# Later chunks of 384 tokens, issued from a second table of steps, in a linear-attention and feed-forward kernel

## The chip, the cores and the metric

The kernel runs on one core of one Trainium2 chip. The core has a matrix engine (PE in the profile; its weight loads are PEld), a vector engine (DVE), a scalar engine (ACT), a general engine (POOL), and SP, which issues most DMAs. Each engine takes its own instructions in order and waits on semaphores for the others. The metric is the device time of one execution in microseconds (us); the median over several runs counts.

## The reference

There are 8 batches of 8 heads, 576 tokens each, head width 64, and 128 random features. All is float32.

```python
def phi(x):
    proj = np.einsum('bhsd,md->bhsm', x, omega)
    sq = np.sum(x * x, axis=-1, keepdims=True) / 2.0
    h = proj - sq
    h = h - np.max(h, axis=-1, keepdims=True)
    return np.exp(h) / np.sqrt(m)
...
kv = np.einsum('bhsm,bhsd->bhmd', k_p, v)
z = np.sum(k_p, axis=2)
num = np.einsum('bhsm,bhmd->bhsd', q_p, kv)
den = np.einsum('bhsm,bhm->bhs', q_p, z)[..., None] + 1e-06
...
h = x @ w_in
g = h - np.tanh(h)
return (g @ w_out)
```

The attention output (4608 tokens by 512) is `x`; `w_in` is 512 by 2048, `w_out` 2048 by 512.

## The kernel before, in words

The 2048 columns between the two weight matrices are cut into 16 slices of 128. Each float32 operand of the large products is kept as a high and a low part of a faster type, and a product is made of three matmuls: high by high, high by low, low by high. For a slice of weights and a chunk of tokens that gives 12 matmuls into `h` (4 blocks of the 512 inputs by 3, line 373) and 3 matmuls for each 128 tokens into the output bank `po` (lines 403 to 405). Between them lies a chain on two engines, the tile's **g chain**: tanh on ACT (`g`, line 379), `h - tanh` on DVE (line 381), the high part on ACT (`gh`, 384), the low part on DVE (`gl`, 387). `g` is one tile; `gh` and `gl` have two buffers.

Tokens are worked in chunks. Chunks 0 and 1 (512 tokens together) form a first stage whose order is written out in a table (`ORDER`, one step per word, each step on one engine). There the weights are also read and decoded. All of this first stage, up to slice 13, stands in that table. The later stage takes slices 14 and 15 of it and then chunks 2 to 17, 256 tokens each: a loop over chunks and over pairs of slices, so that one **unit** is 24 matmuls of 256 columns into one bank `h`, and 12 matmuls of 512 columns into two banks `po`. Units alternate on PE: the 24 matmuls of the next unit stand before the 12 of this one.

Beside it runs the attention for later chunks. A **q unit** (chunk, pair of heads `c`) loads 256 queries, splits them, makes the features (`pj_q`, line 177), the row minima and exponentials, the denominators, turns the result by four transposes (`pt`, line 325), splits it into `qh` on ACT (329) and `ql` on DVE (330), and multiplies by the key-value matrix in the **numerators** (`pn`, lines 336 and 337: for each of two heads one matmul with `qh` and one with `ql`, cut where a batch ends inside the chunk). Then `xs` is put together (340 to 343) and split into the chunk's input `xh` and `xl` (349, 350). A **k unit** (batch, pair of heads) does the same kind of work for the keys of a batch. These units are Python generators; `beat()` advances each by one yield at fixed points of the loop, and the dictionary `start` says at which beat a unit begins. The instructions so emitted are then put in order for each engine by the framework's scheduler. While the banks of the first stage are in use, features, transposes and numerators share one PSUM bank, `pj0`.

Of the kernel before, what the change touches and what calls it, by code (L numbers as in the profile page):

```python
# [78 lines left out]


@with_exitstack
def favor_attention_ffn(ctx: ExitStack, tc: tile.TileContext, qT, kT, va, vt, omT, w, out):
# [77 lines left out]
    def split_rows(x, f):  # L160

        copy(mode["hi"], x[0:D, 0, :], f[0:D])
        copy(mode["hi"], x[D:P, 1, :], f[D:P])
        nc.vector.tensor_sub(x[D:P, 0, :], f[0:D], x[0:D, 0, :].bitcast(F32))
        nc.vector.tensor_sub(x[0:D, 1, :], f[D:P], x[D:P, 1, :].bitcast(F32))

    def features(lhs, name):

# [4 lines left out]
        for g in range(0, n, 2):
            m = min(2, n - g)
            pj = ps.tile([P, 2, 2 * M], F32, tag=bank("pj"), name=f"pj_{name}_{g}")
            for i in range(m):
                nc.tensor.matmul(pj[:, i], lhs[g + i], om2, start=True, stop=True)  # L177
# [13 lines left out]
    def k_unit(b, c):  # L191

        f = att("kf", [P, S], F32, f"kf_{b}_{c}")
        load(f, kT[c, :, b * S : (b + 1) * S])
        yield from k_single(b, c, f)

    def k_single(b, c, f):


        n = f"{b}_{c}"  # L200
        v = att("vr", [P, 9, D], F32, f"v_{n}")
        nc.sync.dma_start(v, vt[b - 2, c])
        yield
        x = att("kx", [P, 2, S], F32R, f"kx_{n}")
        split_rows(x, f)
        yield
        xf = x.rearrange("p h s -> p (h s)")
        tiles = [xf[:, t * P : (t + 1) * P] for t in range(9)]
        pk = ps.tile([P, 2, 2, M], F32, tag=bank("pk"), name=f"pk_{n}")
        zs = att("zs", [P, 2, M], F32, f"zs_{n}")  # L210

        def split(ph, t, n_t):

            ku = []
            for g in range(0, n_t, 2):
                w = min(2, n_t - g)
                k = att("khl", [P, 2, 2, M], F32R, f"khl_{n}_{t + g}")
                u = att("vhl", [P, 2, 2, D], F32R, f"vhl_{n}_{t + g}")
                nc.vector.tensor_copy(k[:, :w, 0], ph[:, g : g + w])  # L219
                nc.gpsimd.tensor_sub(k[:, :w, 1], ph[:, g : g + w], k[:, :w, 0].bitcast(F32))  # L220
                if n_t > 1:
                    parts = [(slice(0, P), slice(0, w), slice(t + g, t + g + w))]
                else:
                    parts = [(slice(D * h, D * h + D), h, t) for h in range(2)]
                    nc.gpsimd.memset(u[0:D, 1].bitcast(F32), 0.0)
                    nc.gpsimd.memset(u[D:P, 0].bitcast(F32), 0.0)
                for p, i, j in parts:
                    nc.gpsimd.tensor_copy(u[p, i, 0], v[p, j])  # L228
                    nc.vector.tensor_sub(u[p, i, 1], v[p, j], u[p, i, 0].bitcast(F32))
                ku += [(k[:, i if n_t > 1 else 0].rearrange("p a m -> p (a m)"),  # L230
                        u[:, i].rearrange("p a d -> p (a d)")) for i in range(2)]
            return ku

        def kv(h, ku, first, last):
            for i, (k, u) in enumerate(ku):
                nc.tensor.matmul(pk[:, h].rearrange("p a m -> p (a m)"), u, k,  # L236
                                 start=first and i == 0, stop=last and i == len(ku) - 1)

        def zsum(ph, h):
            zt = att("c1", [P, 2, M], F32, f"zt_{n}_{h}")  # L240
            nc.gpsimd.tensor_add(zt, ph[:, 0:2], ph[:, 2:4])
            nc.gpsimd.tensor_add(zs[:, h], zt[:, 0], zt[:, 1])

        pa = features(tiles[0:4], f"ka{n}")
        yield
        ku = split(pa, 0, 4)
        zsum(pa, 0)
        yield
        pm = features(tiles[4:5], f"km{n}")
        kv(0, ku, True, False)  # L250
        yield
        km = split(pm, 4, 1)
        yield
        pb = features(tiles[5:9], f"kb{n}")
        kv(0, km[:1], False, True)
        kv(1, km[1:], True, False)
        yield
        zsum(pb, 1)
        nc.gpsimd.tensor_add(zs[0:D, 0], zs[0:D, 0], pm[0:D, 0])
        nc.gpsimd.tensor_add(zs[D:P, 1], zs[D:P, 1], pm[D:P, 0])  # L260
        ku = split(pb, 5, 4)
        yield
        kv(1, ku, False, True)
        zhl = att("khl", [P, 2, 2, M], F32R, f"zhl_{n}")
        nc.vector.tensor_copy(zhl[:, 0], zs)
        nc.gpsimd.tensor_sub(zhl[:, 1], zs, zhl[:, 0].bitcast(F32))
        c1 = att("c1", [P, 2, M], F32, f"c1_{n}")
        nc.scalar.copy(c1, pk[:, :, 0])
        nc.vector.tensor_add(c1, pk[:, :, 1], c1)
        yield  # L270
        for h in range(2):
            nc.tensor.transpose(pk[:, 0, h], c1[:, h], ident)
        for i in range(2):
            nc.tensor.matmul(pk[:, 1].rearrange("p h m -> p (h m)"), ones,
                             zhl[:, i].rearrange("p h m -> p (h m)"), start=i == 0, stop=i == 1)
        kvt = att("kvs", [P, 2, D], F32, f"kvs_{n}")
        nc.scalar.copy(kvt, pk[:, 0, :, D:])
        nc.vector.tensor_add(kvt, pk[:, 0, :, 0:D], kvt)
        zb = att("zb", [P, 2, M], F32, f"zb_{n}")
        nc.scalar.copy(zb, pk[:, 1])  # L280
        w = att("kvw", [P, 4, D], F32R, f"kvw_{n}")
        nc.scalar.copy(w[:, 0::3, :], kvt)
# [139 lines left out]


    need = {b: (b * S) // TC for b in range(B)}
    xdone = {}
    x2 = {}
    gens = []

# [401 lines left out]
```

## Time and profile before

| what | us |
|---|---|
| median of 3 runs | 1056.81 (1055.3 to 1058.27) |
| the profiled execution | 1051.56 |
| its span, first to last instruction | 1049.8 |
| PE busy | 1032.1 |
| DVE busy | 803.9 |
| ACT busy | 678.4 |
| POOL busy | 278.5 |

All times of single instructions come from this one execution. Matmuls overlap, since one starts while the last is still leaving the array, so a matmul's own duration is longer than the distance to the next one; the distance between starts is what a matmul costs a full PE. I call it the pitch.

### The profile page before, as it was taken

The numbers are of one execution on the slowest core, as the hardware profiler recorded it, in microseconds if no ns is written. First come the engines' busy times: TensorE is split into PE (matmuls) and PEld (weight loads), VectorE is DVE, ScalarE is ACT, GpSimd is POOL, SyncE is SP. The second block draws the span as 40 slices with busy tenths as digits, with TensorE's granted clock in tenths as the row PEclk, the third lists the DMA queues.
The fourth block names the chain that finished last, engine by engine and source line by source line (L and its number), as shares of the span: only waits on it lengthen the run. The fifth ranks groups of instructions, "written<-read, shape, count | busy, mean of one in ns | idle before, by whom it ended". The sixth has DMA issues, their size and how long they took to land.

```text
span 1049.8 us, 20079 instructions
## 1 busy us (share of the span) xinstructions
PE 1032.1 (98%) x6908; PEld 935.6 (89%) x6908; DVE 803.9 (77%) x2761; ACT 678.4 (65%) x1730; POOL 278.5 (27%) x445
## 2 busy tenths in 40 slices
PE   8899999989999999999999999999999999999998
PEld 7677888989999999999999998999999999999997
DVE  6997776775788876789889888998888887666522
ACT  7998655664676755676677677676667675555422
POOL 0344760001233310234333323333333341000000
PEclk9999999999999999999999999999999999999999
DMA  8999662010111100010111111111101010100000
GB/s 234 291 249 268 127 156 66 32 41 1 29 54 33 42 23 31 23 53 23 53 29 54 33 54 34 44 39 34 54 24 52 25 40 7 35 12 21 1 21 21
DMA packets 43462, 64.67 MB, mean 62 GB/s; under 512 B 18656, under 2 KB 28000, under 8 KB 41312
## 3 DMA queue, kind: packets, MB, share of 16 engines
q1 hardware_dynamic: 38672, 38.19, 12.4%
q10 hardware_dynamic: 2384, 16.81, 4.6%
q0 software_dynamic: 2304, 8.39, 4.2%
q8 instruction: 55, 0.90, 0.4%
q14 instruction: 47, 0.39, 0.1%
HBM read 45.55 MB, written 9.44 MB: 52 GB/s over the span
## 4 chain that ended last, share of the span: by engine, by line
PE 87%; DVE 4%; ACT 4%; DMA 2%; POOL 1%; issue 1%; ACTq 0%; DVEq 0%; POOLq 0%
PE h L373 37%; PE po L403 11%; PE po L404 11%; PE po L405 11%; PE pj_q L177 3%; PE pt L325 2%; PE pk L236 2%; PE pn L337 2%; PE pn L336 2%; DMA w<-a 2%; ACT k_phi L491 1%; PE pj_ka L177 1%; PE pj_kb L177 1%; DMA q_f<-qT 1%; POOL a L638 1%
## 5 line engine op out<-in xcount | busy, mean ns | idle before, releaser
L373 PE MATMUL h<-xh,w 128*128 128x256 f32 (+1 forms) x2176 | 448.7, 291 | 2.7 <-DMA w<-a 1.9
L373 PEld LDWEIGHTS h<-xh,w 128*128 128x128 f32 x2176 | 355.0, 191 | 12.8 <-DMA w<-a 2.8
L373 PE MATMUL h<-xl,w 128*128 128x256 f32 (+1 forms) x1088 | 316.7, 291 | 1.0 <-DVE xl L350 1.0
L373 PEld LDWEIGHTS h<-xl,w 128*128 128x128 f32 x1088 | 207.7, 191 | 7.4 <-DVE xl L350 1.2
L403 PE MATMUL po<-w,gh 128*128 128x512 f32 x544 | 213.8, 393 | 0.0
L404 PE MATMUL po<-w,gh 128*128 128x512 f32 x544 | 213.4, 392 | 0.0
L405 PE MATMUL po<-w,gl 128*128 128x512 f32 x544 | 211.6, 391 | 0.0
L384 ACT CAST gh<-g 128x512 fp32r<-128x512 f32 x144 | 89.7, 623 | 96.3 <-DVE g L381 93.6
L379 ACT ACTIVATE g<-h 128x512 f32<-128x512 f32 x144 | 85.7, 595 | 95.2 <-PE h L373 84.3
L381 DVE TENSOR_TENSOR g<-h,g 128x512 f32<-128x512 f32 x144 | 98.8, 686 | 61.5 <-ACT g L379 60.2
L387 DVE TENSOR_TENSOR gl<-g,gh 128x512 fp32r<-128x512 f32 x144 | 109.9, 763 | 46.3 <-ACT gh L384 44.3
L405 PEld LDWEIGHTS po<-w,gl 128*128 128x128 f32 x544 | 102.3, 188 | 21.2
L403 PEld LDWEIGHTS po<-w,gh 128*128 128x128 f32 x544 | 102.5, 188 | 16.7 <-issue 0.3
L404 PEld LDWEIGHTS po<-w,gh 128*128 128x128 f32 x544 | 102.5, 188 | 15.5
L185 ACT ACTIVATE phi_q<-phi_q,nb_q 128x128 f32<-128x128 f32 x240 | 78.8, 392 | 4.1 <-DVE nb_q L181 4.0
L220 POOL TENSOR_TENSOR khl<-phi_ka,khl 128x256 fp32r<-128x256 f32 x40 | 31.5, 796 | 176.0 <-DVE khl L219 168.3
L330 DVE TENSOR_TENSOR ql<-pt,qh 128x512 fp32r<-128x512 f32 x60 | 41.2, 686 | 38.2 <-ACT qh L329 38.0
L315 DVE CUSTOM_DVE_ANT_0 junk<-phi_q,zb 128x128 f32<-128x128 f32 (+1 forms) x200 | 59.9, 300 | 11.6 <-DVE dn L315 0.5
L181 DVE CUSTOM_DVE_ANT_0 phi_q<-pj_q,phi_q 128x128 f32<-128x128 f32 x240 | 55.9, 283 | 7.2 <-ACT phi_q L178 7.2
L638 POOL TENSOR_SCALAR a<-a 128x1024 f32<-128x1024 f32 x14 | 53.9, 3852 | 20.8 <-ACT a L627 14.4
L329 ACT CAST qh<-pt 128x512 fp32r<-128x512 f32 x60 | 34.9, 582 | 37.7 <-PE pt L325 37.5
L228 POOL CAST vhl<-v 128x128 fp32r<-128x128 f32 (+1 forms) x120 | 37.7, 314 | 78.6 <-PE pk L236 73.1
(158 smaller groups left out, 1835.9 us busy)
## 6 DMA issues: line engine op xcount, KB each, us to landing
raw<-w ACTq DMA_DIRECT2D x16, 1024.0 KB, 6.0
out<-o SPq DMA_DIRECT2D x36, 256.0 KB, 2.0
w<-a POOLq DMA_DIRECT2D x16, 512.0 KB, 6.1
qf<-qT SPq DMA_DIRECT2D x60, 128.0 KB, 2.1
kf<-kT SPq DMA_DIRECT2D x20, 288.0 KB, 2.8
v<-vt SPq DMA_DIRECT2D x20, 288.0 KB, 2.8
v<-va SPq DMA_DIRECT2D x12, 320.0 KB, 4.9
k_f<-kT SPq DMA_DIRECT2D x12, 288.0 KB, 4.3
```

The lines of the kernel that those rows point to most:

```text
L181: nc.vector.tensor_tensor_reduce(ph[:, j], pj[:, i, :M], ph[:, j], scale=-SCALE, scalar=3.0e38, op0=ALU.add, op1=ALU.min, accum_out=nb[:, ...
L185: nc.scalar.activation(ph[:, j], ph[:, j], AF.Exp, bias=nb[:, j : j + 1], scale=-1.0)
L315: nc.vector.tensor_tensor_reduce(bank("junk")[r], ph[r, i], kvs[b, c][1][r, h], scale=1.0, scalar=EPS, op0=ALU.mult, op1=ALU.add, accum_ou ...
L373: nc.tensor.matmul(o, w_, x, start=i == 0, stop=i == len(prods) - 1)
L379: nc.scalar.activation(g, p, AF.Tanh)
L381: nc.vector.tensor_sub(g, p, g)
L384: nc.scalar.copy(gh, g)
L387: nc.vector.tensor_sub(gl, g, gh.bitcast(F32))
L403: nc.tensor.matmul(po[t], h, wt[f][:, 0, DM:], start=first, stop=False)
L404: nc.tensor.matmul(po[t], h, wt[f][:, 1, DM:], start=False, stop=False)
L405: nc.tensor.matmul(po[t], l, wt[f][:, 0, DM:], start=False, stop=last)
L638: engine.tensor_scalar(u["af"], u["af"], -TOP, TOP, op0=ALU.max, op1=ALU.min)
```

## The change

From token 768 on, chunks hold 384 tokens instead of 256: 10 chunks of 384 in place of 15 of 256, while chunk 2 keeps its 256. A unit of such a chunk is one slice: 12 matmuls of 384 columns into `h` and 9 of 512 columns into three banks `po`. A q unit has 384 queries: six features, two banks of three transposes, and numerators of 384 columns. Generators, beats and the scheduler are gone from the later stage. All its steps stand in a second table, `LATER`, of some 4200 words in the order of a list scheduling, and each engine takes its instructions in that order. The table also names the PSUM bank of each product. Several small tiles (`g`, `gh`, `gl`, `xs`, the output's copies) become fixed places in three larger ones, `zf`, `zr` and `xb`; the inputs of odd and even chunks lie in `xa` and `xb`.

```diff
+TW = 384
+START = [0, TC, 2 * TC, *range(3 * TC, NT, TW)]
+NCH = len(START)
...
+LATER = """
+x.h0 q30.ld f0d.o0 x.h1 x.l0 x.h2 x.l1 f0e.h0.6 x.h3 x.l2 x.l3 f0e.h1 q30.sa f0d.o1 q30.sv f0e.th f0d.o2 f0e.g q31.ld
...
+fce.th fcd.o1 fce.g fce.gh fcd.o2 fce.gl fcf.h0.7 fcf.h1 fce.o0 fcf.th fce.o1 fcf.g fcf.gh fce.o2 fcf.gl fcf.o0 fcf.o1
+sc.c0.0 fcf.o2 sc.d0 sc.c1.0 sc.d1 sc.c2.0 sc.d2
...
+    def slices_of(ch, s):
+        return (2 * s, 2 * s + 1) if ch == 2 else (s,)
...
+            for i, (w_, x) in enumerate(prods):
+                if ch == 2 or half is None or half == i // 6:
+                    nc.tensor.matmul(o, w_, x, start=i == 0, stop=i == len(prods) - 1)
...
+        def turned(slot, h):
+            u["pt", h] = ps.tile([P, TW], F32, tag=BANKS[slot], name=f"pt_{n}_{h}")
+            for t in range(WB):
+                nc.tensor.transpose(u["pt", h][:, t * P : (t + 1) * P], u["ph"][:, 2 * t + h], ident)
+
+        def q_hi(h):
+            u["qh", h] = ak.tile([P, TW], F32R, tag="qh", name=f"qh_{n}_{h}")
+            nc.scalar.copy(u["qh", h], u["pt", h])
+
+        def q_lo(h):
+            u["ql", h] = ak.tile([P, TW], F32R, tag="ql", name=f"ql_{n}_{h}")
+            nc.vector.tensor_sub(u["ql", h], u["pt", h], u["qh", h].bitcast(F32))
+
+        def numerators(slot, h):
+            u["pn", h] = ps.tile([P, TW], F32, tag=BANKS[slot], name=f"pn_{n}_{h}")
+            for b, s, e in pieces:
+                w = kvs[b, c][0][:, h * P : (h + 1) * P]
+                nc.tensor.matmul(u["pn", h][:, s:e], w, u["qh", h][:, s:e], start=True, stop=False)
+                nc.tensor.matmul(u["pn", h][:, s:e], w, u["ql", h][:, s:e], start=False, stop=True)
...
+    def f_unit(ch, s):
+        u = {}
+        n = 4 if ch < 3 else WB
+        g = zf[:, 0:n]
+        gh, gl = (zr[:, k + s % 2 * 4 : k + s % 2 * 4 + n] for k in (0, 8))
...
+    def issue(order, makers):
+        units = {}
+        for token in order.split():
             name, step_, *slot = token.split(".")
             if name not in units:
                 units[name] = makers[name[0]](*(int(x, 16) for x in name[1:]))
             units[name][step_](*(int(x) for x in slot))
...
+    with tc.manual_schedule():
+        issue(ORDER, dict(k=native_k, q=native_q, d=decoder, f=feed))
...
+        issue(LATER, dict(k=k_unit, q=q_unit, f=f_unit, s=s_unit, x=x2_unit))
```

In the table `f3a.h0` and `f3a.h1` are the first and last six matmuls into `h` of chunk 3, slice 10; `th`, `g`, `gh`, `gl` its chain and `o0` to `o2` its output blocks. `q31.z0`, `a0`, `l0`, `m0` are the transposes, `qh`, `ql` and numerators of the first head of pair 1 in chunk 3.

The order on PE at three places. First, where chunk 3 begins. In the order before, `pt_3` are the transposes of pair 3 of chunk 3, `po` the outputs of chunk 2, and `h_0` the first unit of chunk 3:

```order
L403 MATMUL po_2_1991<-w_1638,gh_6_2454 128x512
L404 MATMUL po_2_1991<-w_1638,gh_6_2454 128x512
L325 MATMUL pt_3_2272<-ident,phi_q_3_2147 128x128 x4
L405 MATMUL po_2_1991<-w_1638,gl_6_2456 128x512
L403 MATMUL po_2_1991<-w_1682,gh_6_2454 128x512
L404 MATMUL po_2_1991<-w_1682,gh_6_2454 128x512
L405 MATMUL po_2_1991<-w_1682,gl_6_2456 128x512
L373 MATMUL h_0_2574<-xh,w_508 128x256
L373 MATMUL h_0_2574<-xl,w_508 128x256
```

The order after on PE at the same place, from the numerators of pair 3, second head (`pn_3_1`), to the first unit of chunk 3; between the rows shown stand the 12 matmuls of `po_0` and `po_1` with `w_1608` and `w_1649`:

```order
L625 MATMUL pn_3_1_2625<-qh_3_1_2585,k_kvw 128x384
L626 MATMUL pn_3_1_2625<-ql_3_1_2603,k_kvw 128x384
L698 MATMUL pk_1_2634<-khl_1_A_2560,vhl_1_A_2484 128x256 x2
L458 MATMUL pj_k_1_M<-om,kx_1_2338 128x256
L570 MATMUL po_0_2045<-w_1608,zr 128x512
...
L698 MATMUL pk_1_2634<-khl_1_A_2628,vhl_1_A_2600 128x256 x2
L458 MATMUL pj_k_1_B_2675<-om,kx_1_2338 128x256 x2
L458 MATMUL pj_k_1_B_2679<-om,kx_1_2338 128x256 x2
L547 MATMUL h_0_2684<-xa,w_508 128x384 x6
L698 MATMUL pk_1_2634<-khl_1_M,vhl_1_M 128x256 x2
L547 MATMUL h_0_2684<-xa,w_508 128x384 x6
```

All numerators of chunk 3 now stand ahead of its first unit, with 12 output matmuls between; before, the transposes of the last pair stood just ahead of it.

Second, between transposes and numerators of a q unit. In the order before on PE, the transposes of pair 0 of the next chunk, where fewest matmuls follow them before the numerators (which come 21 rows below the transposes):

```order
L325 MATMUL pt_0_2509<-ident,phi_q_0_2401 128x128 x4
L373 MATMUL h_0_2574<-xh,w_508 128x256
L373 MATMUL h_1_2665<-xh,w_743 128x256
L373 MATMUL h_0_2574<-xl,w_508 128x256
L373 MATMUL h_0_2574<-xh,w_508 128x256
L373 MATMUL h_0_2574<-xh,w_1068 128x256
L373 MATMUL h_0_2574<-xl,w_1068 128x256
```

The order after on PE, pair 1 of chunk 3, where fewest follow (`pt_1_0` and `pt_1_1` are the transposes of its two heads):

```order
L611 MATMUL pt_1_0_2152<-zf,phi_q_1_1942 128x128 x3
L611 MATMUL pt_1_1_2159<-zf,phi_q_1_1942 128x128 x3
L570 MATMUL po_1_2070<-w_743,zr 128x512
L571 MATMUL po_1_2070<-w_743,zr 128x512
L572 MATMUL po_1_2070<-w_743,zr 128x512
L570 MATMUL po_1_2070<-w_782,zr 128x512
L571 MATMUL po_1_2070<-w_782,zr 128x512
L572 MATMUL po_1_2070<-w_782,zr 128x512
L625 MATMUL pn_1_0_2178<-qh_1_0_2163,k_kvw 128x384
L626 MATMUL pn_1_0_2178<-ql_1_0_2174,k_kvw 128x384
```

The numerators of a head have moved up to directly behind nine short rows; the work of a whole unit no longer lies between.

Third, the last chunk, on PE in the order after, from the 12 matmuls of slice 14 to the outputs of slice 13 and the matmuls of slice 15:

```order
L547 MATMUL h_14_11859<-xa,w_1708 128x384 x3
L547 MATMUL h_14_11859<-xb,w_1708 128x384 x9
L570 MATMUL po_0_11530<-w_1649,zr 128x512
L571 MATMUL po_0_11530<-w_1649,zr 128x512
L572 MATMUL po_0_11530<-w_1649,zr 128x512
L570 MATMUL po_1_11536<-w_1649,zr 128x512
L571 MATMUL po_1_11536<-w_1649,zr 128x512
L572 MATMUL po_1_11536<-w_1649,zr 128x512
...
L547 MATMUL h_15_11885<-xa,w_1740 128x384 x3
L547 MATMUL h_15_11885<-xb,w_1740 128x384 x9
L570 MATMUL po_0_11530<-w_1708,zr 128x512
```

The alternation of units is kept, but between a unit's `h` and its `po` stand 9 matmuls of 512 columns and 12 of 384, where 12 of 512 and 24 of 256 stood.

More of the change, by code (lines that the diff above doesn't have):

```diff
@@ L188, in favor_attention_ffn @@
     kvf = {}
     kvs = {}
[L191 to L282, printed above, removed]
-        nc.vector.tensor_sub(w[:, 1:3, :], kvt, w[:, 0::3, :].bitcast(F32))
-        kvs[b, c] = (w.rearrange("p a d -> p (a d)"), zb)
@@ new lines, in ffn_g, with ffn_out @@
+    def ffn_g(ch, s, p):
+        n = 4 if ch < 3 else WB
+        p = blocks(p)[:, 0:n]
+        g = zf[:, 0:n]
+        gh, gl = (zr[:, k + s % 2 * 4 : k + s % 2 * 4 + n] for k in (0, 8))
+        nc.scalar.activation(g, p, AF.Tanh)
+        yield
+        nc.vector.tensor_sub(g, p, g)
+        yield
+        nc.scalar.copy(gh, g)
+        yield
+        nc.vector.tensor_sub(gl, g, gh.bitcast(F32))
+        yield gh, gl
+    def ffn_out(ch, s, gh, gl, only=None):
+        po = pos[ch]
+        for t in range(len(po)) if only is None else (only,):
+            for j, f in enumerate(slices_of(ch, s)):
+                first, last = f == 0, f == NF - 1
+                nc.tensor.matmul(po[t], gh[:, 2 * j + t], wt[f][:, 0, DM:], start=first, stop=False)
+                nc.tensor.matmul(po[t], gh[:, 2 * j + t], wt[f][:, 1, DM:], start=False, stop=False)
+                nc.tensor.matmul(po[t], gl[:, 2 * j + t], wt[f][:, 0, DM:], start=False, stop=last)
@@ L395, in ffn_out @@
-    def ffn_out(ch, s, gh, gl):
-        po = pos[ch]
-        for t in range(len(po)):
-            for j in ((t // 2,) if ch == 0 else range(2)):
-                f = s if ch == 0 else 2 * s + j
-                h = gh[:, j, t % 2 * P : (t % 2 + 1) * P]
-                l = gl[:, j, t % 2 * P : (t % 2 + 1) * P]
-                first, last = f == 0, f == NF - 1
-                nc.tensor.matmul(po[t], h, wt[f][:, 0, DM:], start=first, stop=False)
-                nc.tensor.matmul(po[t], h, wt[f][:, 1, DM:], start=False, stop=False)
-                nc.tensor.matmul(po[t], l, wt[f][:, 0, DM:], start=False, stop=last)
@@ new lines, in q_unit @@
+        st = dict(ld=ld, sa=sa, sv=lambda: split_lo(u["x"], u["f"]), xh=lambda: x_hi(ch, c, xs), xl=lambda: x_lo(ch, c, xs))
+        for t in range(WB):
+            lhs = lambda t=t: [u["x"][:, h, t * P : (t + 1) * P] for h in range(2)]
+            st.update(pair(u, str(t), lhs, 2 * t, f"q{n}", lambda slot: ak.tile([P, 2 * WB, M], F32, tag=f"phq{slot}", name=f"phi_q{n}")))
+            st[f"d{t}"] = partial(den, t)
+        for h in range(2):
+            for k, f in dict(n=norm, z=turned, a=q_hi, l=q_lo, m=numerators, ta=x_part, tv=x_sum).items():
+                st[f"{k}{h}"] = partial(f, h=h)
@@ L420, in out_tiles @@
-    def out_tiles(ch, tags=("po0", "po1")):
-        pos[ch] = [ps.tile([P, DM], F32, tag=t, name=f"{t}_{ch}") for t in tags]
[L424 to L427, printed above, removed]
-    def tick(new=(), force=False):
-        assert gens or not force
-        gens[:] = [g for g in gens if next(g, gens) is not gens]
-        for kind, i, c in new:
-            gens.append((k_unit if kind == "k" else q_unit)(i, c))
-            next(gens[-1])
+                nc.vector.tensor_copy(u[t], blocks(pos[ch][t]))
+            else:
+                nc.scalar.copy(u[t], blocks(pos[ch][t]))
@@ L438, in tile_at, with send, x2_unit @@
+        def send(t):
+            r = START[ch] + t * P
+            nc.sync.dma_start(blocks(out[r : r + P, :]), u[t])
+        st = {}
+        for t in range(4):
+            st.update({f"c{t}": partial(copy_out, t=t), f"d{t}": partial(send, t)})
+        return st
+    def x2_unit():
+        st = {}
+        for c in range(NC):
+            st.update({f"h{c}": lambda c=c: x_hi(2, c, x2[c]), f"l{c}": lambda c=c: x_lo(2, c, x2[c])})
+        return st
     def tile_at(kind, slot, shape, dtype, name):
```

719 lines of the change are left out of this document (520 added, 199 removed).

## Prediction

> **What bounds the kernel now.** I read the page's busy line first, then the windows (busy time of each engine in stretches), the chain that ended last, and PE's timeline where a window is not full.
>
> ```profile
> span 1049.8 us, 20079 instructions
> PE 1032.1 (98%) x6908; PEld 935.6 (89%) x6908; DVE 803.9 (77%) x2761; ACT 678.4 (65%) x1730; POOL 278.5 (27%) x445
> ```
>
> The windows; columns: stretch, length, busy us of PE, PEld, DVE, ACT, POOL, then PE's granted clock.
>
> ```profile
> 150.00:200.00 50.00, 50.00 (x291) 44.10 (x290) 33.44 (x106) 30.57 (x69) 3.31 (x5) 1.00 0.23 60
> 200.00:250.00 50.00, 47.32 (x304) 42.85 (x303) 35.92 (x129) 28.22 (x71) 2.95 (x4) 0.97 0.07 24
> 250.00:300.00 50.00, 50.00 (x345) 46.44 (x345) 33.56 (x111) 28.35 (x71) 12.24 (x28) 1.00 0.09 29
> 600.00:650.00 50.00, 49.31 (x336) 45.32 (x335) 41.54 (x160) 32.90 (x87) 19.99 (x38) 1.00 0.14 44
> 950.00:1000.00 50.00, 50.00 (x334) 46.00 (x333) 28.53 (x90) 24.14 (x56) 0.00 (x0) 1.00 0.03 11
> ```
>
> The later stage starts near 155 us. PE is full there, idle for 2.68 us in 200 to 250 and 0.69 us in 600 to 650. A busy PE need not be PE at its pitch, so I look at the pitch where nothing but units runs, in the last chunk. Two pieces of the chain (start, length):
>
> ```profile
> 1020.79 2.87 PE h L373 x24
> 1026.41 2.87 PE h L373 x24
> ```
>
> 24 matmuls of 256 columns take 2.87 us: a pitch of 0.1196. From one such piece to the next is 5.62 us; the 12 output matmuls of 512 columns take the other 2.75: 0.2292 each. The groups of that width hold 3072 matmuls, 192 for each of 16 chunks, with next to no idle ahead of them:
>
> ```profile
> L373 PE MATMUL h<-xh,w 128*128 128x256 f32 x2048 | 407.3, 284 | 0.7 <-ACT xh L349 0.7
> L373 PE MATMUL h<-xl,w 128*128 128x256 f32 x1024 | 291.8, 285 | 1.0 <-DVE xl L350 1.0
> ```
>
> The window from 200 is the exception. PE's timeline there, at the start of chunk 3 (start, length, in brackets the idle before and what ended it):
>
> ```profile
> 228.12 0.28 PE L373 MATMUL h<-xh,w 128*128 128x256 f32 x1
> 228.88 0.92 PE L177 MATMUL pj_q<-om,qx 128*128 128x256 f32 x4 [0.48 <-DVE qx L164]
> 230.28 0.63 PE L325 MATMUL pt<-ident,phi_q 128*128 128x128 f32 x4 [0.48 <-DVE xs L343]
> 231.64 0.50 PE L373 MATMUL h<-xh,w 128*128 128x256 f32 x2 [0.74 <-ACT xh L349]
> 233.13 0.58 PE L373 MATMUL h<-xl,w 128*128 128x256 f32 x1 [0.98 <-DVE xl L350]
> 233.51 0.63 PE L373 MATMUL h<-xh,w 128*128 128x256 f32 x2
> ...
> 236.05 0.28 PE L373 MATMUL h<-xh,w 128*128 128x256 f32 x1
> ```
>
> Between 228.12 and 236.05 stand 1 + 15 matmuls of `h`, 4 of `pj_q` (20 at 0.12) and 4 transposes (0.35, below): 2.75 us of work in 7.93. The stall costs 5.2 us: 2.68 idle, the rest slow matmuls behind it (0.21 apart from 233.51). So the kernel is bound by the sum of PE's pitches, plus this stall.
>
> **The change part by part, against the profiled execution (1051.56).**
>
> *Matmuls into `h`.* Chunks 3 to 17 have 15 x 192 = 2880 matmuls of 256 columns; at 0.1196 that is 344.4 us. The new chunks have 10 x 192 = 1920 of 384 columns, a width that the trace lacks. In proportion to the 256 row a pitch is at most 1.5 x 0.1196 = 0.1794 (344.5 us, no gain); in proportion to the 512 row at least 0.75 x 0.2292 = 0.1719 (330.0 us, 14.4 gained). I take the middle of the two widths, 0.1744: 334.8 us, **9.6 us gained**, since 0.1096 for 256 more columns is a steady 0.43 ns a column above a fixed part of some 10 ns. All of it lies on the path.
>
> [...]
>
> *Output matmuls* keep number and width (three for each slice and 128 tokens). *Features, transposes, k units* keep their counts too; only their place moves.
>
> *Numerators.* A q unit whose chunk lies in one batch has 4 matmuls of 256, a cut one 8 smaller ones. First rows and the row that follows, of one of each kind:
>
> ```profile
> 706.80 0.28 PE L336 MATMUL pn<-qh,kvw 128*128 128x256 f32 x1
> 707.28 0.40 PE L403 MATMUL po<-w,gh 128*128 128x512 f32 x1
> 345.05 0.25 PE L336 MATMUL pn<-qh,k_kvw 128*128 128x192 f32 x1
> 345.41 0.34 PE L336 MATMUL pn<-qh,k_kvw 128*128 128x192 f32 x1
> 345.59 0.27 PE L337 MATMUL pn<-ql,k_kvw 128*128 128x192 f32 x1
> 345.70 0.21 PE L336 MATMUL pn<-qh,kvw 128*128 128x64 f32 x1
> 345.86 0.72 PE L177 MATMUL pj_ka<-om,kx 128*128 128x256 f32 x4
> ```
>
> Whole 0.48, cut 0.81, a pair of 192 columns 0.29. Batch ends (multiples of 576) cut 5 of the 15 old chunks and 3 of the 10 new ones. Before: 40 units x 0.48 + 20 x 0.81 = 35.4. After: 28 x 4 x 0.1744 + 12 x 4 x 0.29 = 19.5 + 13.9 = 33.4. **2.0 us gained.**
>
> *The old stall.* In the order before, the transposes of pair 3 stand just ahead of chunk 3's first unit, and all of that unit's inputs come late through the one bank `pj0`. In the order after, 12 output matmuls, 6 of `pk`, `pj` and so on stand between the last numerators and that unit: 12 x 0.2292 + 9 x 0.12 = 3.8 us, and its second half, which alone needs pair 3, comes 6 x 0.1744 = 1.0 us later. What must happen meanwhile is `xs` (ACT, DVE), `xh`, `xl`. The rows:
>
> ```profile
> L349 ACT CAST xh<-xs 128x256 fp32r<-128x256 f32 x60 | 24.5, 408 | 21.7 <-DVE xs L343 21.4
> L350 DVE TENSOR_TENSOR xl<-xs,xh 128x256 fp32r<-128x256 f32 x60 | 25.7, 429 | 3.6 <-ACT xh L349 3.3
> ```
>
> Four such steps at 0.42, half as wide again, make some 2.1 us. I take the 5.2 us as **gone**; what is late next is counted under new stalls.
>
> *New waits.* Every step that PE waits for now stands in a fixed order, with less PE work to cover it. The rows of the chains:
>
> ```profile
> L379 ACT ACTIVATE g<-h 128x512 f32<-128x512 f32 x144 | 85.7, 595 | 95.2 <-PE h L373 84.3 <-DVE gl L387 4.8 <-DVE ql L330 3.0
> L384 ACT CAST gh<-g 128x512 fp32r<-128x512 f32 x144 | 89.7, 623 | 96.3 <-DVE g L381 93.6 <-PE pt L404 1.3
> L381 DVE TENSOR_TENSOR g<-h,g 128x512 f32<-128x512 f32 x144 | 98.8, 686 | 61.5 <-ACT g L379 60.2
> L387 DVE TENSOR_TENSOR gl<-g,gh 128x512 fp32r<-128x512 f32 x144 | 109.9, 763 | 46.3 <-ACT gh L384 44.3
> L329 ACT CAST qh<-pt 128x512 fp32r<-128x512 f32 x60 | 34.9, 582 | 37.7 <-PE pt L325 37.5
> L330 DVE TENSOR_TENSOR ql<-pt,qh 128x512 fp32r<-128x512 f32 x60 | 41.2, 686 | 38.2 <-ACT qh L329 38.0
> 701.43 0.60 PE L325 MATMUL pt<-ident,phi_q 128*128 128x128 f32 x4
> 701.78 0.48 PE L373 MATMUL h<-xh,w 128*128 128x256 f32 x2
> ```
>
> The g chain takes at most 0.60 + 0.69 + 0.62 + 0.76 = 2.67 us (384 columns take less than these 512). Its cover shrinks from 5.62 to 9 x 0.2292 + 12 x 0.1744 = 4.16: enough. Transposes cost 0.35 for four and end 0.25 later. `qh` and `ql` at 384 columns, halfway between the 256 rows above and these, take 0.50 + 0.56, so the numerators are ready 1.31 us after the transposes. Before, the cover was 5 us as a rule (701.78 to 706.80). Now it is 0.26 + 6 x 0.2292 = 1.64 at the tightest place and, by the order with these pitches, 2.6 for the median of 40. Each cover exceeds its bare chain; a stall needs another instruction ahead in ACT's or DVE's queue. DVE work is the same within a few us (1.5 times as wide, two thirds as many), so it stays below PE (41.5 of 50 where it is busiest among the windows above). The cost of new stalls lies between 0 and the old stalls' size several times over; I take **4 us**, near the 5.9 (5.2 + 0.69) that the old order left.
>
> *First stage and end* stay: the same table, and three output tiles instead of two are copied behind the last matmul. The last g chain has 2.06 us of cover plus 0.46 before `gl`: 0.2 us at most.
>
> **Sum:** 9.6 + 2.0 + 5.2 - 4 = 12.8 us less: 1051.6 becomes 1038.8. The runs' median, 1056.8, stands 5.2 above the profiled execution; I keep that distance: **1044.0 us**.
>
> **The rivals.**
>
> *Width gives nothing.* The 384 pitch is 0.1794. For it speaks that only two widths are seen; against it that 512 columns cost less than twice 256. Then 1044.0 + 9.6 = 1053.6. [...]
>
> *The chunk-start stall comes back.* A chunk start needs four pairs' `xl` in time; by the order, 3.8 and 3.6 us of PE work cover the last pair at the first two starts, more at the later ones. Two stalls of 5.2 in place of my 4 us: 1044.0 + 6.4 = 1050.4. For it: the old order stalled with work between, too. Against: the chains fit the covers, and features have more banks.
>
> *Slower: numerators late everywhere.* If at each head's transposes ACT or DVE still holds one more instruction of 0.69 us (the `g` rows), `ql` ends at 2.0 us, 0.36 behind the tightest cover. With 10 x 4 x 2 = 80 heads that is 29 us in place of 4: 1044.0 + 25 = 1069. It decides from (9.6 + 2.0 + 5.2) / 80 = 0.21 us each. For it: DVE can be late, as here, where `gl` takes 1.24 instead of 0.76 beside POOL:
>
> ```profile
> 702.36 0.73 POOL L220 TENSOR_TENSOR khl<-phi_kb,khl 128x256 fp32r<-128x256 f32 x1
> 702.40 1.24 DVE L387 TENSOR_TENSOR gl<-g,gh 128x512 fp32r<-128x512 f32 x1 [0.33 <-ACT gh L384]
> ```
>
> Against: the median cover of 2.6 takes such a delay without a stall. [...]
>
> That the change doesn't do what it says I exclude: the order shows the 384-wide forms.
>
> **How the numbers follow.** Forecast 0.65, width 0.10, chunk starts 0.17, numerators 0.08. The range reaches down to the full 14.4 us of width and no new stall (1044.0 - 4.8 - 4 = 1035) and up to the width rival, 1054. No change can be told within 0.3%, 3.2 us. The forecast is faster throughout; width half faster, half the same; chunk starts faster in 0.15 of 0.17; numerators slower in 0.06, the same in 0.02. Faster 0.85, same 0.09, slower 0.06.
>
> **What would show it.** The 384 groups of `h` with starts 0.174 apart; PE full in every window from 155 us; no idle row at chunk 3's start; idle before `pn` and `po` a few us in all. I am wrong if starts are 0.18 apart, or if PE waits for `ql`, `xl` or `gl` for over 17 us in all.

## The result, and the profile after

The median over seven runs is 1050.15 us (1045.88 to 1052.76), against 1056.81 for the kernel before (seven runs beside it): 0.9929 of it, 95% interval 0.9905 to 0.9952, so 0.7% faster. The profiled execution took 1046.16 us, 5.4 less than the one before; the forecast was 12.8 less. The direction and the range held; of the gain about half is there. The page of the changed kernel:

```profile
span 1044.3 us, 17933 instructions
PE 1025.6 (98%) x5836; PEld 917.1 (88%) x5836; DVE 810.4 (78%) x2761; ACT 686.1 (66%) x1730; POOL 278.1 (27%) x445
```

PE is busy for 6.5 us less and the span is 5.5 shorter. The windows show how the loss is spread now (columns as before):

```profile
150.00:200.00 50.00, 48.99 (x276) 42.09 (x277) 36.56 (x124) 33.85 (x80) 7.91 (x12) 1.00 0.27 73
200.00:250.00 50.00, 49.43 (x311) 45.35 (x310) 46.20 (x166) 35.68 (x91) 18.04 (x37) 1.00 0.15 47
250.00:300.00 50.00, 49.41 (x278) 45.41 (x277) 43.30 (x162) 35.79 (x96) 16.59 (x35) 1.00 0.09 27
...
600.00:650.00 50.00, 49.95 (x285) 45.65 (x284) 43.68 (x171) 34.59 (x90) 16.17 (x31) 1.00 0.09 27
```

The one hole of 2.68 us at chunk 3 is gone; in its place most windows between 200 and 800 us miss 0.2 to 0.8 us, and behind that PE is full. PE's timeline where chunk 3 begins now has no idle row:

```profile
231.65 0.63 PE L458 MATMUL pj_k_B<-om,kx 128*128 128x256 f32 x4
232.12 1.21 PE L547 MATMUL h<-xa,w 128*128 128x384 f32 x6
233.17 0.40 PE L698 MATMUL pk<-khl_M,vhl_M 128*128 128x256 f32 x2
233.41 1.23 PE L547 MATMUL h<-xa,w 128*128 128x384 f32 x6
234.47 0.64 PE L458 MATMUL pj_q<-om,qx 128*128 128x256 f32 x4
```

The pitch of 384 columns is read from the chain in the last chunk, as the 256 pitch was:

```profile
1021.35 2.12 PE h L547 x12
...
1025.53 2.12 PE h L547 x12
```

Twelve matmuls take 2.12 us, 0.1767 each. In proportion to the 256 row it would be 0.1794: there is a gain, but of 0.0027 a matmul, not of the 0.0050 that I had taken.

Some steps of the attention that come up from here on. The tail of a k unit, in its order: DVE makes `c` (step `cv`, line 725), the sum of two parts of its key-value products; PE turns `c` and sums the keys' features over the partitions (`kt`, lines 729 and 731); ACT copies the results out of PSUM (`ka`, `zb`); DVE adds to the first (`kb`, 763); ACT and DVE split that into a high and a low part (`wa`, and `wv`, 747). `zl` (718) is the low part of the key sums, on POOL; `d` (598) is a step of a q unit's denominators, on DVE.

Where PE waits in the later stage, from the list of its waits (us in total, times, longest; waits under some 0.15 are not listed):

```profile
PE pk L729 <- DVE c L725: 2.3, 5, 0.6
...
PE pt L611 <- DVE phi_q L606: 1.0, 2, 0.6
PE pn L625 <- DVE ql L619: 0.7, 1, 0.7
```

Idle rows are only part of it. Summing along PE's timeline, row by row, the distance to the next start minus the pitches of the row, the stalls come to some 11 us: 4.1 at `kt` (line 729, nine places), 1.9 at `pt`, 2.2 at `pn`, about 1 at the `pk` of line 698, the rest a few tenths each. One of them in full, on three engines:

```profile
263.21 0.73 POOL L718 TENSOR_TENSOR zhl<-zf,zhl 128x256 fp32r<-128x256 f32 x1 [1.64 <-DVE zhl L715]
...
263.42 0.67 DVE L598 CUSTOM_DVE_ANT_0 zf<-phi_q,k_zb 128x128 f32<-128x128 f32 x1
...
263.97 0.40 PE L458 MATMUL pj_q<-om,qx 128*128 128x256 f32 x2
264.02 0.07 DVE L598 DVE_READ_ACCUMULATOR2_ANT dn<- 128x1 f32 x1
264.02 0.55 DVE L784 TENSOR_TENSOR zf<-h,zf 128x384 f32<-128x384 f32 x1
264.49 0.41 DVE L725 TENSOR_TENSOR c<-pk,c 128x256 f32<-128x256 f32 x1
...
264.96 0.44 PE L729 MATMUL pk<-zf,c 128*128 128x128 f32 x2 [0.59 <-DVE c L725]
```

`d` (line 598) takes 0.67 us instead of 0.29 while POOL's `zl` runs; `g` and `c` behind it on DVE are late by as much, and the transposes `kt`, which the table puts on PE just where `c` should end, wait 0.59, of which 0.38 is this delay. This is the theory that the runs test: the width, the numerators and the old stall give what they give, and about 11 us go back in small stalls, because the fixed order leaves some DVE steps no cover and DVE is slowed beside POOL.

### The profile page after: what moved, and what is told of

Read it like the earlier page. It is cut to its first block, busy times and chain, and to the rows that moved or that the text cites. A ratio compares the mean times of both kernels' runs of the same rounds, so it can differ in the third digit from the quotient of the medians.

```text
span 1044.3 us, 17933 instructions
## 1 busy us (share of the span) xinstructions
PE 1025.6 (98%) x5836; PEld 917.1 (88%) x5836; DVE 810.4 (78%) x2761; ACT 686.1 (66%) x1730; POOL 278.1 (27%) x445
## 4 chain that ended last, share of the span: by engine, by line
PE 77%; DVE 11%; ACT 7%; issue 2%; POOL 2%; DMA 1%; ACTq 0%; DVEq 0%; POOLq 0%
PE h L547 31%; PE po L570 10%; PE po L571 10%; PE po L572 10%; PE pt L611 2%; PE pj_q L458 2%; PE pk L698 2%; POOL a L1012 2%; PE pn L625 1%; PE pn L626 1%; DVE zf L598 1%; ACT k_phi L869 1%; DVE a L1024 1%; DVE a L1032 1%; PE pj_k_B L458 1%
## 5 line engine op out<-in xcount | busy, mean ns | idle before, releaser
L547 PE MATMUL h<-xa,w 128*128 128x384 f32 (+1 forms) x1392 | 288.2, 345 | 0.0
L547 PEld LDWEIGHTS h<-xa,w 128*128 128x128 f32 x1392 | 244.3, 188 | 15.2 <-DVE q_dn L940 0.2
L570 PE MATMUL po<-w,zr 128*128 128x512 f32 x544 | 218.0, 401 | 0.1
L572 PE MATMUL po<-w,zr 128*128 128x512 f32 x544 | 213.6, 393 | 0.6 <-DVE zr L562 0.6
L571 PE MATMUL po<-w,zr 128*128 128x512 f32 x544 | 213.6, 393 | 0.0
L547 PE MATMUL h<-xb,w 128*128 128x384 f32 (+1 forms) x912 | 170.2, 327 | 0.0
L783 ACT ACTIVATE zf<-h 128x384 f32<-128x384 f32 (+1 forms) x170 | 84.3, 496 | 129.6 <-PE h L547 122.9
L784 DVE TENSOR_TENSOR zf<-h,zf 128x384 f32<-128x384 f32 (+1 forms) x170 | 95.7, 563 | 83.2 <-ACT zf L783 81.7
L547 PEld LDWEIGHTS h<-xb,w 128*128 128x128 f32 x912 | 151.1, 188 | 0.2
L786 DVE TENSOR_TENSOR zr<-zf,zr 128x384 fp32r<-128x384 f32 (+1 forms) x170 | 103.2, 607 | 28.0 <-ACT zr L785 26.0
L785 ACT CAST zr<-zf 128x384 fp32r<-128x384 f32 (+1 forms) x170 | 88.3, 519 | 54.3 <-DVE zf L784 52.8
L572 PEld LDWEIGHTS po<-w,zr 128*128 128x128 f32 x544 | 102.1, 188 | 24.5 <-DVE zr L562 1.6
L570 PEld LDWEIGHTS po<-w,zr 128*128 128x128 f32 x544 | 102.4, 188 | 12.2 <-ACT zr L560 0.5
L571 PEld LDWEIGHTS po<-w,zr 128*128 128x128 f32 x544 | 102.5, 188 | 10.9
```

The lines of the kernel that those rows point to most:

```text
L547: nc.tensor.matmul(o, w_, x, start=i == 0, stop=i == len(prods) - 1)
L570: nc.tensor.matmul(po[t], gh[:, 2 * j + t], wt[f][:, 0, DM:], start=first, stop=False)
L571: nc.tensor.matmul(po[t], gh[:, 2 * j + t], wt[f][:, 1, DM:], start=False, stop=False)
L572: nc.tensor.matmul(po[t], gl[:, 2 * j + t], wt[f][:, 0, DM:], start=False, stop=last)
L783: th=lambda: nc.scalar.activation(g, blocks(u["p"])[:, 0:n], AF.Tanh),
L784: g=lambda: nc.vector.tensor_sub(g, blocks(u["p"])[:, 0:n], g),
```

## The experiments

The times of the runs on other chips go by the ratio to the kernel before, run beside them. As the first stage varies by some us between executions (last section), the later stage is also given by itself: from the end of the last 512-column `h` of the first stage to the end of the last `po`, on PE's timeline. It took 879.9 us before and 870.1 after; 3.2 us of the difference is work that the second table puts ahead of that point. The second execution of the changed kernel in the table gives 870.4, so that a difference of a few tenths says nothing. The others are compared with this one, which I call the base.

| kernel | ratio to before (95%) | later stage, us |
|---|---|---|
| after, again | 0.992 (0.9892 to 0.9948) | 870.4 |
| `c` one DVE step sooner | 0.9902 (0.9877 to 0.9927) | 869.3 |
| POOL cut short | 0.9842 (0.9819 to 0.9864) | 859.4 |
| before, POOL cut short | 0.9994 (0.9966 to 1.0022) | 878.4 |
| key split off POOL | 0.9989 (0.9965 to 1.0012) | 874.1 |
| `kt` later | 1.005 (1.0023 to 1.0076) | 881.1 |
| `kt` and followers later, first try | 1.0047 (1.003 to 1.0065) | 881.6 |
| the same as a whole | 0.9969 (0.9944 to 0.9993) | 872.9 |
| followers bunched | 1.005 (1.0021 to 1.0079) | 879.7 |
| framework's order | 1.1592 (1.1549 to 1.1634) | 1046.6 |

**The width by itself.** Both kernels without their later attention. In the kernel before:

```diff
+    start.clear()
...
-            while ch > 2 and xdone.get(ch, 0) < NC:
-                tick((), True)
```

and in the changed one:

```diff
+        nc.vector.memset(xb[0][:, 8 * TC :].bitcast(F32), 0.0)
-        issue(LATER, dict(k=k_unit, q=q_unit, f=f_unit, s=s_unit, x=x2_unit))
+        issue(" ".join(x for x in LATER.split() if x[0] not in "qk"), dict(k=k_unit, q=q_unit, f=f_unit, s=s_unit, x=x2_unit))
```

> The kernel before without any attention step of the later stage (no q units, no k units): only the units of 24 matmuls into `h` and 12 into `po` are left, and chunks from 2 on work on old data. It is the base for the same cut of the changed kernel; the difference of the two is the worth of the width alone. Theory (narrower sum of pitches): 15 x 8 units of 5.62 us, 674.4 us for the chunks from 3 on, PE full in every window from 200 us, starts in `h` 0.1196 apart, starts in `po` 0.2292. Rival (part of PE's time in the whole kernel is interference by the attention work): starts closer than 0.1196.

> The changed kernel without any attention step of the later stage: only units of 12 matmuls of 384 columns into `h` and 9 into `po`; chunks from 2 on work on old data. Theory: 10 x 16 units of 4.18 us, 668.8 us, so 5.2 to 5.6 us less than the same cut of the kernel before, with no idle time of PE: the width is worth 5, not the 9.6 predicted. Rival (the 384 pitch of 0.1744 holds when nothing disturbs, and 0.1767 is the attention's interference): 9.6 us less. Rival (the width gives nothing): no difference.

Measured: two units in a row on the chain, of the kernel before

```profile
863.87 2.87 PE h L373 x24
869.49 2.87 PE h L373 x24
```

and of the changed kernel

```profile
863.62 2.12 PE h L547 x12
867.80 2.12 PE h L547 x12
```

From start to start 5.62 and 4.18: 120 x 5.62 = 674.4 against 160 x 4.18 = 668.8, so 5.6 us, with PE full from 200 us on in both. The 384 pitch is 0.1767 also with nothing beside it, so the attention does not make it; the width is worth 5.2 to 5.6. The spans do not show it (898.7 and 899.3), since in the second run the first stage ended 8.1 us later: 4.1 as in the whole kernels, the rest at least in part from a late load at its start (PE stands 3.7 us for it, 1.3 in the first run).

**The order by the framework.** `LATER` issued outside the manual order:

```diff
+    close_pool("a0")
...
+    issue(LATER, dict(k=k_unit, q=q_unit, f=f_unit, s=s_unit, x=x2_unit))
```

> The changed kernel, its steps of the later stage unchanged, but issued outside the manual order, so that the framework's scheduler orders each engine. Theory (the width and the numerators give some 10 us whoever orders; the table removes the 5.2 us stall and brings about 10 us of small ones): the width's gain stays, so within 10 us of the changed kernel, and its idle rows stand at other steps than `kt`, `pt` and `pn`. Rival (the table is what makes the gain): as slow as the kernel before, 1056, or slower. Rival (the order is where the gain was lost, and the scheduler's own has thicker cover): 1044 or less.

Measured: 1227.63, 17% slower than the table. My theory's number (within 10 us) was far off; the rival that the table makes the gain possible holds, for these steps. Four windows:

```profile
300.00:350.00 50.00, 40.07 (x180) 33.32 (x179) 35.40 (x142) 30.39 (x79) 9.78 (x20) 0.80 0.13 40
400.00:450.00 50.00, 42.80 (x214) 37.49 (x213) 36.99 (x141) 30.32 (x78) 12.56 (x25) 0.86 0.14 43
450.00:500.00 50.00, 50.00 (x273) 45.65 (x272) 36.55 (x124) 27.48 (x72) 14.12 (x26) 1.00 0.09 26
500.00:550.00 50.00, 40.11 (x183) 34.24 (x182) 35.14 (x131) 29.58 (x77) 13.90 (x29) 0.81 0.12 36
```

In the first PE stands for 10 of 50 us, between 330 and 343 on waits of 0.3 to 2.1 us for POOL and DVE one after another, and the granted clock (third figure from the end) falls to 0.80; in the third neither happens. So these steps, with their fixed places and banks, keep PE full only in an order made for them; whether steps of this width laid out otherwise would need one was not tried. Two rows of PE in the first window:

```profile
332.67 0.50 PE L698 MATMUL pk<-khl_B,vhl_B 128*128 128x256 f32 x2 [2.10 <-POOL khl_B L671]
334.16 1.29 PE L458 MATMUL pj_q<-om,qx 128*128 128x256 f32 x4 [0.98 <-DVE qx L447]
```

The matmuls themselves are slower there too: the four at 334.16 take 1.29 us, where the row of four at 234.47 above takes 0.64. In these windows the clock is 0.80 to 0.86 where PE stands for 7 to 10 of 50 us, and 1.00 where it is full; what lowers it, the runs do not show.

**Covering `kt`.** Two edits of the table against the largest group of stalls. First, `kt` behind the next output step:

```diff
-        issue(LATER, dict(k=k_unit, q=q_unit, f=f_unit, s=s_unit, x=x2_unit))
+        issue(put_off(LATER, ("kt",)), dict(k=k_unit, q=q_unit, f=f_unit, s=s_unit, x=x2_unit))
```

> The changed kernel with one edit of the table: each `kt` of a k unit (its transposes, which wait for the sum `c` of DVE) stands behind the next step of output matmuls, which covers it by at least 0.69 us. Theory (small stalls where a DVE step has no cover): the nine stalls at `kt`, 4.1 us in all, go, and 2 to 4 us of them come off the time: 1046 to 1048 for the median, 1042 to 1044 for a run at full clock. Rival (a stall that is taken away comes back at the next thin place): 1050, with the idle time at `pt`, `pn` or `h` instead. Rival (the new place of `kt` makes the steps behind it late): above 1050.

Second, `c` one DVE instruction sooner, with the unchanged kernel beside it as the base:

```diff
+        issue(sooner(LATER, ("cv",), 1), dict(k=k_unit, q=q_unit, f=f_unit, s=s_unit, x=x2_unit))
```

> The changed kernel once more, unchanged, as the base for the three beside it on this chip. Expected: 0.993 of the kernel before, and the same small stalls at the same steps (`kt` behind DVE's `c` at some nine places), since each engine's order is fixed.

> The changed kernel with one edit of the table: the sum `c` of each k unit, for which its transposes on PE wait, stands one DVE instruction earlier (ahead of a `g`, `gl`, `n`, `t` or `d` step of another unit). Theory (PE waits where DVE's step ends too late, and DVE is late by one slowed instruction): most of the 4.1 us of stalls at `kt` go, little comes elsewhere, 2 to 4 us off the later stage. Rival (the stall moves to the step that now stands behind `c`): no difference within 1 us, with the idle time at other steps.

Measured: with `c` sooner the stalls at `kt` fall from 4.3 to 0.6 us, but those at `pt` rise from 2.1 to 3.4 and others a little:

```profile
PE pt L611 <- DVE phi_q L606: 1.5, 3, 0.9
```

The later stage is 1.1 us shorter, and the medians (1048.68 and 1048.93) cannot be told apart. The rival is nearer: the waits have moved to steps that now stand behind `c`. With `kt` later the stalls at `kt` are gone too, but the later stage is 10.7 us longer than in the base. What happened is on DVE's timeline:

```profile
310.52 1.03 DVE L606 TENSOR_TENSOR phi_q<-phi_q,dn 128x384 f32<-128x384 f32 x2
312.05 0.29 DVE L763 TENSOR_TENSOR zf<-pk,zf 128x128 f32<-128x128 f32 x1 [0.50 <-ACT zb L738]
312.71 0.29 DVE L747 TENSOR_TENSOR kvw<-zf,kvw 128x128 fp32r<-128x128 f32 x1 [0.36 <-ACT kvw L743]
312.92 0.28 DVE L469 CUSTOM_DVE_ANT_0 phi_q<-pj_q,phi_q 128x128 f32<-128x128 f32 x1
```

and on PE's:

```profile
311.74 0.40 PE L572 MATMUL po<-w,zr 128*128 128x512 f32 x1
313.56 0.30 PE L611 MATMUL pt<-zf,phi_q 128*128 128x128 f32 x1 [1.42 <-DVE nb_q L469]
```

The followers `kb` (763) and `wv` (747), held up with their unit, now stand on DVE directly behind `kt`'s results; each waits there for ACT's step that has only just been issued, 0.86 us together; over the whole run DVE waits 11.5 us at `kb` and 1.5 at `wv`, against 0.2 and 0.4 in the unchanged kernel. The row minima (469) behind them are late, and PE, which waits for them before `pt`, stands 1.42 us. Three more runs take this apart. Moving the six last steps of a unit:

```diff
+        issue(later_by_one(LATER, ("kt", "ka", "zb", "kb", "wa", "wv")), ...)
```

> The changed kernel with one edit of the table: each of the last six steps of a k unit (`kt`, `ka`, `zb`, `kb`, `wa`, `wv`) stands behind the next output step after its old place, so that the whole tail is later and keeps about its own distances; putting `kt` alone later cost 11 us of the later stage. Theory (there the followers of `kt` on ACT and DVE stood directly behind it, blocked their queues, and held up the query features that came after them): with the distances kept most of the 11 us comes back, within 4 us of the changed kernel. Rival (a later `kt` is itself what costs, because the next steps need its bank or its result): 8 us or more slower than the changed kernel, as before.

Measured: 1.0047, as with `kt` alone, so the rival's number. But the edit let several followers go at the same output step, so that they stood as close as in the run before; it did not separate the two. The next two do: `kt` and all followers moved by the same number of places, and `kt` left alone with its followers bunched at the place of `kb`:

```diff
+        issue(moved(LATER, ("kt", "ka", "zb", "kb", "wa", "wv")), ...)
...
+        issue(bunched(LATER, ("ka", "zb", "kb", "wa", "wv")), ...)
```

> The changed kernel with the tail of each k unit (`kt`, `ka`, `zb`, `kb`, `wa`, `wv`) moved back as a whole: `kt` stands behind the next output step, and each follower is moved by as many places as `kt`. The two shifts before this one put several followers at the same place behind `kt`, so that `kb` waited on DVE for ACT's `zb`, and `wv` for `wa`, with query features queued behind them; the second shift therefore did not keep the distances as its expectation said. Theory (the bunching cost the 11 us, not the later `kt`): within 4 us of the changed kernel, ratio 0.989 to 0.996, the stalls at `kt` gone. Rival (a later `kt` costs by itself): ratio 1.000 or above.

> The changed kernel with `kt` at its old place and its five followers bunched: `ka`, `zb`, `kb`, `wa`, `wv` directly behind one another at the place of `kb`. Theory (DVE's fixed queue blocked by `kb` and `wv`, each waiting for ACT's step just issued, holds up the row minima and with them PE): DVE idles before `kb` and `wv` in each of 20 units, 5 to 12 us slower than the changed kernel, ratio 0.997 to 1.005, with PE waiting at `pt` and `pn`; the stalls at `kt` stay. Rival (the bunching is harmless): ratio 0.992.

Measured: moved as a whole, the later stage is 2.4 us longer than the base instead of 11, the `kt` stalls gone and 4 us more at `pt`; the ratio, 0.9969, is a little above what I had named. Bunched alone, it is 9.3 us longer, with `kt`'s stalls as they were (4.5 us). A row of DVE's waits, which in the unchanged kernel counts one time and 0.4 us:

```profile
DVE kvw L747 <- ACT kvw L743: 7.3, 20, 0.4
```

Once in each of 20 units DVE stands 0.36 us at `wv` for a step that ACT was given just before. Before `kb` it stands only three times, 1.1 us in all, so that half of the mechanism named did not show here. The theory's main point holds: bunching alone costs 9.3 us, of the 10.7 that the later `kt` had cost.

**DVE beside POOL.** POOL's subtractions and additions of the later stage on 8 of 128 columns (this leaves most low parts of the keys' features and most of the key sums out; their tiles are made once and set to zero), first in the changed kernel:

```diff
-            nc.gpsimd.tensor_sub(k[:, :m, 1], u["ph" + g[0]][:, t : t + m], k[:, :m, 0].bitcast(F32))
+            nc.gpsimd.tensor_sub(k[:, :m, 1, 0:8], u["ph" + g[0]][:, t : t + m, 0:8], k[:, :m, 0, 0:8].bitcast(F32))
...
-            nc.gpsimd.tensor_add(zt, ph[:, 0:2], ph[:, 2:4])
+            nc.gpsimd.tensor_add(zt[:, :, 0:8], ph[:, 0:2, 0:8], ph[:, 2:4, 0:8])
```

> The changed kernel with POOL's subtractions and additions of the later stage (low parts of the keys' features, key sums and their low parts) working on 8 columns instead of 128, the tiles otherwise zero; so most of those low parts and sums are left out of the result, and the steps, their order and their waits stay. Theory (DVE is slowed while POOL works, and PE's small stalls are those of late DVE steps): the slowed DVE instructions, 39 us of extra time, nearly go; the stalls at `kt` and part of those at `pt` and `pn` go with them; 4 to 8 us less than the changed kernel. Rival (the stalls come from the order alone, whatever POOL does): no difference within 2 us, with PE's idle time at the same steps.

Measured: 0.9842, and the later stage 11.0 us shorter than the base. The page:

```profile
PE 1020.8 (98%) x5836; PEld 920.0 (89%) x5836; DVE 771.9 (74%) x2763; ACT 686.4 (66%) x1730; POOL 175.3 (17%) x445
```

DVE does the same work in 38.5 us less than on the page of the changed kernel above (810.4). The windows:

```profile
200.00:250.00 50.00, 50.00 (x321) 46.20 (x320) 43.69 (x171) 37.74 (x98) 9.06 (x36) 1.00 0.16 49
250.00:300.00 50.00, 50.00 (x284) 46.23 (x283) 41.31 (x168) 35.50 (x95) 9.73 (x37) 1.00 0.10 27
300.00:400.00 100.00, 100.00 (x574) 92.30 (x573) 82.58 (x334) 71.27 (x185) 14.90 (x60) 1.00 0.12 37
```

PE is full, with the same instructions in the same order; of the stalls at `kt`, `pt` and `pn` some 0.5 us is left, and one of 0.6 in front of line 458, for ACT, stays. So the order alone makes next to none of the small stalls; the order and POOL's work together make nearly all. The cut has a second effect, since POOL's own results also come sooner (it is busy for 175.3 us in place of 278.1). In the list of PE's waits of the unchanged kernel none is for POOL; but about 1 of the 11 us stood at the `pk` of line 698, which reads POOL's low parts, and for that part the run does not tell the two apart. The same cut in the kernel before:

```diff
-                nc.gpsimd.tensor_sub(k[:, :w, 1], ph[:, g : g + w], k[:, :w, 0].bitcast(F32))
+                nc.gpsimd.tensor_sub(k[:, :w, 1, 0:8], ph[:, g : g + w, 0:8], k[:, :w, 0, 0:8].bitcast(F32))
```

> The kernel before with the same cut as made in the changed one: POOL's subtractions and additions of the later stage work on 8 columns instead of 128 (most low parts of the keys' features and most of the key sums are left out of the result). In the changed kernel that took 11 us off the later stage and all of DVE's slowed instructions with it. Theory (slowed DVE instructions cost PE only where the order leaves thin cover; before, a whole unit of 5 us lay between): DVE's 31 us of extra time go, the time falls by 0 to 3 us, at most the 5 of its one large stall. Rival (the contention costs any order alike, so it says nothing on the change): 8 to 11 us less than the kernel before.

```profile
PE 1033.4 (98%) x6908; PEld 937.2 (89%) x6908; DVE 776.5 (74%) x2764; ACT 683.1 (65%) x1730; POOL 174.8 (17%) x445
```

DVE is 27 us shorter here too (803.9 before), and the time does not change: 0.9994; the later stage is 1.5 us shorter. The old stall at chunk 3 stands as it was:

```profile
235.34 0.50 PE L375 MATMUL h<-xh,w 128*128 128x256 f32 x2 [0.74 <-ACT xh L351]
237.01 0.39 PE L375 MATMUL h<-xl,w 128*128 128x256 f32 x1 [1.16 <-DVE xl L352]
```

So contention that costs DVE 27 us costs the old order 1.5, and contention that costs DVE 38.5 us costs the new one 11. This fits the covers: in the old order some 5 us of PE work lay behind DVE's steps as a rule, and the change took much of that away.

**Work taken off POOL.** The point suggests a kernel that beats both, with nothing left out: ACT makes the high parts of the keys' features, DVE the low parts.

```diff
-            nc.vector.tensor_copy(u["k" + g][:, :m, 0], u["ph" + g[0]][:, t : t + m])
+            nc.scalar.copy(u["k" + g][:, :m, 0], u["ph" + g[0]][:, t : t + m])
...
-            nc.gpsimd.tensor_sub(k[:, :m, 1], u["ph" + g[0]][:, t : t + m], k[:, :m, 0].bitcast(F32))
+            nc.vector.tensor_sub(k[:, :m, 1], u["ph" + g[0]][:, t : t + m], k[:, :m, 0].bitcast(F32))
```

> The changed kernel with the split of the keys' features moved off POOL: ACT makes the high parts (DVE did), DVE the low parts (POOL did); the table is unchanged and nothing is left out. 100 casts move from DVE to ACT (some 28 us), 100 subtractions from POOL to DVE (some 38 us by the `c` rows of 0.41, less 27 us of casts). Theory (what costs is DVE slowed beside POOL): POOL's busy time falls by some 75 us, about half of DVE's slowed instructions go, 2 to 6 us less than the changed kernel. Rival (what costs is any step that the table's model did not place): the moved steps now hold up ACT's and DVE's fixed queues, no gain, or some us slower.

Measured: 0.9989. Two lists of waits, PE's and DVE's:

```profile
PE pk L729 <- DVE c L725: 3.7, 6, 0.9
...
DVE khl_B L671 <- ACT khl_B L667: 5.9, 9, 1.6
DVE khl_A L671 <- ACT khl_A L667: 2.8, 4, 1.5
```

POOL's busy time fell by 68 us and DVE's by 10, and the DVE instructions of the later stage that are over 0.15 us above their usual time fell from 120 to 66, as the theory had it; but the later stage is 3.7 us longer than the base, with more waiting at `kt` (5.2 us of stalls). The rival holds: DVE's low parts (line 671) stand at places that were chosen for POOL's, and there they wait 8.7 us in all for ACT's high parts (667), with all that stands behind them on DVE. A table made anew for this division of work, or for DVE's real durations, was not tried. No version that leaves nothing out beats the changed kernel by more than its measurement is uncertain.

## Why the prediction was right or wrong

- **What bounds it** (the sum of PE's pitches plus stalls): right. With the stalls taken away by the cut in POOL's work, PE is full and only its sum is left. The sign that PE would be full in every window did not hold; no start in `h` is 0.18 apart, and the waits stayed far under 17 us, so neither sign of being wrong came.
- **`h` matmuls, 9.6 us:** right in sign, too large. The pitch is 0.1767, inside the bounds of 0.1719 and 0.1794 but above my 0.1744; 1920 x 0.1767 = 339.3, so 5.2 less than 344.4; the cut kernels gave 5.6. The three widths are not on a straight line: 0.0571 for the first 128 columns more, 0.0525 for the next. Why is open.
- **Numerators, 2.0 us:** too small. Summed over their rows on PE's timeline, to the start of the next row, they took 36.1 before and 30.9 after, with some of the stalls among them; with POOL cut short it is 29.9. So 5.2 to 6 are gained. The mistake is the 0.29 for a pair of 192 columns: four such matmuls take 0.43, so a pair 0.21, as the other head of the same piece would have told (in the kernel before, a pair runs from 345.05 to the row at 345.25).

```profile
321.52 0.25 PE L625 MATMUL pn<-qh,k_kvw 128*128 128x192 f32 x1
...
321.95 0.42 PE L570 MATMUL po<-w,zr 128*128 128x512 f32 x1
```

- **The old stall, 5.2 us:** right, gone, and nothing late in its place at chunk 3. (Beside the 12 output matmuls the cover has 9 short ones, as in the sum; the words said 6.) The rival of a stall at every chunk start did not happen.
- **New waits, 4 us:** the step that failed. They are 11. I had put the g chains, the numerators and the chunk starts beside their covers and found each cover longer than its chain, and that was right for the bare chains: with POOL cut short they do not stall. Two things were missed. The k units were passed over with "keep their counts too; only their place moves", and there stands the largest group, `kt`, with no cover at all behind `c`. And I had the row of DVE slowed beside POOL (`gl` at 1.24), but used it only for a rival about the numerators, not as a cost that falls on every thin cover; the run of the kernel before with POOL cut short shows that the old order hid nearly all of it.
- **The slower rival** (numerators late everywhere): its place was wrong, 2.2 us at `pn` in place of 25, but its mechanism, DVE late by one instruction beside POOL, is what cost.

Together: 5.2 + 5.2 to 6 + 5.2, some 16, gained, and the new stalls are 11 where the old order had some 2 besides its large one. That makes 7 us; measured were 9.8 in the later stage less the 3.2 that moved ahead of it, 6.6, and 5.4 to 6.7 for the whole execution. That no more than half of the forecast was missed is in part luck: the numerators gave 3 to 4 us more than their term, which nearly covers the 4.4 that the width gave less. That the first stage ends some 1 us later than the moved work explains was not followed up.

## What to carry to other kernels

An order that is fixed for all engines pays by tight covers, and they are only as good as the durations it was made with: mark each place where PE follows a DVE or ACT step with less than one slowed instruction of slack (`d` lost 0.38 us at the stall shown), and count those places, before trusting the bare chains. Contention that changes next to nothing in a loose order can take much of a gain in a tight one (1.5 us of the later stage before, 11.0 after), so undo it in both. When a step of such an order is moved, its followers have to keep their distance (moved as a whole the later stage was 2.4 us longer, with `kt` alone 10.7); of two dependent steps issued next to each other on two engines, the second holds up all that stands behind it on its engine (`wv`, by 0.36 us in each of 20 units).
